# A recurrent attention step: heads 16 to 31 taken ahead of the queries of heads 0 to 15, and a filler unit dealt to four places

## The chip, the cores and the metric

The kernel runs on one core of a Trainium2 chip. The metric is the device time of one execution in microseconds; the median of three runs of the kernel before is 2796.26 us.

## The reference, cut to what matters

Four layers follow each other, A, B, A, B, each added to a residual stream of 2048 tokens by 640. The change is in layer B:

```python
for s in range(n_seg):                       # 64 segments of 32 tokens
    h = jnp.concatenate([mem, xs], axis=1)   # 8 memory tokens, 32 of the segment
    q, k, v = (jnp.einsum('btd,dhe->bhte', h, W) for W in (Wq, Wk, Wv))   # 32 heads of 128
    scores = jnp.einsum('bhqe,bhke->bhqk', q, k) * scale
    scores = jnp.where(mask[None, None], scores, -1000000000.0)
    p = _softmax(scores, axis=-1)
    o = jnp.einsum('bhqk,bhke->bhqe', p, v)
    o = jnp.einsum('bhte,hed->btd', o, Wo)
    mem = o[:, :M, :].copy()                 # the next segment's memory
```

The segments depend on each other through `mem`, so the 64 steps of a layer run one after the other.

## The kernel before

**What a step projects.** Step s of layer B works with 32 columns: the 8 memory tokens of segment s and the first 24 tokens of segment s+1. `thin_mm` multiplies them with half of a weight matrix (16 heads, 2048 columns): 5 chunks of the model dimension times 4 column tiles of the array, 20 matmuls with 32 stationary columns and 512 moving ones. A step has six such groups: Ka and Qa (keys and queries of heads 0 to 15), Kb and Qb (heads 16 to 31), Va and Vb. The last 8 tokens of each segment, its tail, are projected ahead for eight segments at a time: `tail_unit` multiplies 8 heads' weights (128 stationary columns, whole array) with 64 tail tokens, 5 matmuls a head and 40 a unit, and one unit is done in each step for a later group of segments. `tail_evac` (ScalarE) scales and writes it out to a table in HBM, `b_QKd`, from which `tails_load` takes a segment's tails back a step ahead; GpSimd (`tails_copy`) puts them into `QZ` and `KT`. `vtail_unit` and `vtail_evac` do the same for values in 20 thin matmuls, through `b_VTd`.

**From projections to scores.** `kq` evacuates a projection from PSUM to SBUF (ScalarE for Ka, Kb and Qb, VectorE for Qa), `transp4` turns it by four full-array matmuls against the identity (tiles b_TPak, b_TPaq, b_TPbk, b_TPbq), and two copies spread it: `scatter` on VectorE takes the 8 memory columns into `KT[s]` or `QT[s]`, `x_scatter` on ScalarE the 24 others into those of step s+1. `mask_mm` starts a score tile with the additive mask (one full-array matmul). There are two tiles: SPa (b_SP0) with 8 groups of 40 keys, 0 to 3 for the tail queries of all 32 heads, 4 to 7 for heads 0 to 15, and SPb (b_SP1) with groups 8 to 11 for heads 16 to 31. `scores` adds 16 matmuls for heads 0 to 15, 32 small ones for the tail queries, 16 for heads 16 to 31.

**Softmax and after.** Maxima, subtraction, sums, reciprocal and the products `Px` run on VectorE, the exponentials on ScalarE, `Pm` on GpSimd. TensorE meanwhile does Va, Vb, sometimes the LayerNorm transposes of a later block (`ln_spread`, b_lntps), and 30 matmuls of the tail unit. Then `p_transp` turns the probabilities (b_PTP), 10 more tail matmuls follow, `pv` multiplies with the values (b_OTP), `o_mm` with the output weights (b_OPS, and b_OPSd for rows put off from earlier segments, in two parts before and behind b_OPS). The new memory goes through `b_msb` (ScalarE) and b_MT (TensorE) into the 8 memory columns of `b_HX` of the next step (VectorE), with vtail matmuls between.

**Order and buffers.** The order of instructions on TensorE, ScalarE, VectorE and GpSimd is that of the program text: `_OrdNC` ties each instruction to the one before on its engine. SyncE, which starts the transfers, is not tied. PSUM has eight banks: pool `pp` has five buffers in rotation for all tiles made by `ps_tile`, pool `po` one each for the tags tail, ops and opsd. b_TPbq uses the tail buffer of `po`, as does the tail unit later in the step. Line 101 is the wrapper in `_OrdNC` through which every instruction of layer B goes, so the profile's rows are told apart by tiles.

Of the kernel before, what the change touches and what calls it, by code (L numbers as in the profile page):

```python
# [18 lines left out]
F32 = mybir.dt.float32  # L19
BF16 = mybir.dt.bfloat16  # L20
ACT = mybir.ActivationFunctionType
ALU = mybir.AluOpType
AX = mybir.AxisListType
# [6 lines left out]
NCH = 5  # L30
# [568 lines left out]
def layer_B(nc, tc, C, W, x_src, xb_src, x_dst, mem0, B_Wv, B_Wo, nsteps=64, out_bf16=False, tag=""):  # L599
    SCB = 1.0 / math.sqrt(128.0)  # L600
    nc_raw = nc
    nc = _OrdNC(tc, nc_raw, engines=ORDER_ENGINES)
    NG = nsteps // 4
    NT = nsteps // 8
    QKd = tc.dram_tile([nsteps, 128, 512], BF16, name=f"b_QKd{tag}")
    VTd = tc.dram_tile([nsteps, 8, 4096], BF16, name=f"b_VTd{tag}")
    with ExitStack() as ctx:
# [19 lines left out]
        po = psum("b_po", 1)  # L627

        def ps_tile(shape, dtype, name):
            return pp.tile(shape, dtype, name=name, tag="ps")  # L630
# [80 lines left out]
                return HXz[:, :, 0, :]  # L711
            return HX[u // 4][:, :, u % 4, :]

        def thin_mm(cols_ap, Wt, b, name):
            ps = ps_tile([128, 512], F32, name)
            for c in range(NCH):
                for j in range(4):
                    n = 4 * b + j
                    nc.tensor.matmul(ps[32 * j:32 * j + 32, :], lhsT=cols_ap[:, c, :], rhs=Wt[:, c, 512 * n:512 * n + 512],
                                     start=(c == 0), stop=(c == NCH - 1), tile_position=(0, 32 * j), skip_group_check=True)  # L720
            return ps

        def transp4(sb, name, tp=None):
            if tp is None:
                tp = ps_tile([128, 4, 128], BF16, name)
            for i in range(4):
                nc.tensor.transpose(tp[:, i, :], sb[:, 128 * i:128 * i + 128], C.identb[:])
            return tp

        def scatter(eng, tp, b, dst_t, t0, t1, c0):  # L730
            src = tp[:].rearrange("p i (j t) -> p i j t", j=4)[:, :, :, t0:t1]
            dst = dst_t[:, 16 * b:16 * b + 16, c0:c0 + (t1 - t0)].rearrange("p (j i) c -> p i j c", j=4)
            evac(eng, dst, src)
# [20 lines left out]

        tail_ps = {}

        def tail_unit(T, k, i0, i1, shared=False):
            proj, hg = divmod(k, 4)
            Wt = W.wk if proj else W.wq
            if i0 == 0:  # L760
                if shared:
                    tail_ps[0] = ps_tile([128, 8, 64], F32, "b_tail")
                else:
                    tail_ps[0] = po.tile([128, 8, 64], F32, name="b_tail", tag="tail")
            ps = tail_ps[0]
            for i in range(i0, i1):
                h = 8 * hg + i
                for c in range(NCH):
                    nc.tensor.matmul(ps[:, i, :], lhsT=Wt[:, c, 128 * h:128 * h + 128], rhs=TX[T][:, c, :, :].rearrange("p s t -> p (s t)"),
                                     start=(c == 0), stop=(c == NCH - 1))  # L770

        def tail_evac(T, k, eng, home=None):
            proj, hg = divmod(k, 4)
# [52 lines left out]
            for c in range(NCH):  # L826
                nc.sync.dma_start(HX[0][:, c, 1, 0:8], mem0[:, 128 * c:128 * c + 128].rearrange("t p -> p t"))
        for k in range(8):
            tail_unit(0, k, 0, 8, shared=True)
            tail_evac(0, k, "act" if k % 2 == 0 else "dve", (kqp, "kq"))  # L830
            if k % 4 == 1 and 2 + k // 4 < n0:
                ln_norm(2 + k // 4)
            if k % 4 == 3 and 2 + k // 4 < n0:
                ln_spread(ln_ready.pop(0))
# [21 lines left out]
            evac("act" if b == 0 else "dve", Vth[:, b, :], ps[:])  # L856
        vtails_in(0)
        if NT > 1:
            tail_unit(1, 0, 0, 8, shared=True)
            tail_evac(1, 0, "act")  # L860
            vtail_evac(1, 0, vtail_unit(1, 0), "dve")

# [51 lines left out]
        for s in range(nsteps):  # L914
# [13 lines left out]
            def x_scatter(tp, b, D_):  # L928
                if not last:
                    scatter("act", tp, b, D_[s + 1], 8, 32, 8 if D_ is KT else 0)  # L930

            def kq(ps, eng, scale=None):
                sb = kqp.tile([128, 512], BF16, name="b_kq", tag="kq")
                evac(eng, sb[:], ps[:], scale)
                return sb
# [3 lines left out]
            def mask_mm(a):  # L939
                g0, g1 = GR[a]  # L940
                SP = ps_tile([128, g1 - g0, 40], F32, f"b_SP{a}")
                nc.tensor.matmul(SP[:].rearrange("p g k -> p (g k)"), lhsT=C.identb[:], rhs=mask12[:, g0:g1, :].rearrange("p g k -> p (g k)"),
                                 start=True, stop=False, skip_group_check=True)
                return SP

            def scores(SPs):
                for b in range(2):
                    for j in range(4):
                        for i in range(4):
                            h = 16 * b + 4 * j + i  # L950
                            nc.tensor.matmul(SPs[b][32 * i:32 * i + 32, j + 4 * (1 - b), :], lhsT=QT[s][:, h, :], rhs=KT[s][:, h, :],
                                             start=False, stop=True, tile_position=(0, 32 * i), skip_group_check=True)
                    if b == 0:
                        qz = QZ[s % 2][:].rearrange("p x c -> p (x c)")
                        for j in range(4):
                            for e in range(2):
                                for t4 in range(4):
                                    pr = 8 * (t4 // 2) + 2 * j + t4 % 2
                                    nc.tensor.matmul(SPs[0][32 * t4:32 * t4 + 16, j, :], lhsT=qz[:, 24 * pr + 8 * e:24 * pr + 8 * e + 16],
                                                     rhs=KT[s][:, 2 * pr + e, :],  # L960
                                                     start=False, stop=True, tile_position=(0, 32 * t4), skip_group_check=True)

            negmax = sm.tile([128, 12], F32, name="b_negmax", tag="negmax")
            ssum = sm.tile([128, 12], F32, name="b_ssum", tag="ssum")
            rs = sm.tile([128, 12], F32, name="b_rs", tag="rs")
            E_ = wk.tile([128, 12, 40], BF16, name="b_E", tag="E0")

            def soft_max(a, SP):
                nc.vector.tensor_reduce(out=negmax[:, slice(*GR[a])], in_=SP[:], axis=AX.X, op=ALU.max, negate=True)

            def soft_sub(a, SP):
                n_ = GR[a][1] - GR[a][0]
                nc.vector.tensor_tensor(out=SP[:], in0=SP[:], in1=negmax[:, slice(*GR[a])].unsqueeze(2).to_broadcast([128, n_, 40]), op=ALU.add)

            def soft_exp(a, SP):
                nc.scalar.activation(out=E_[:, slice(*GR[a]), :], in_=SP[:], func=ACT.Exp)

            def soft_sum(a):
                nc.vector.tensor_reduce(out=ssum[:, slice(*GR[a])], in_=E_[:, slice(*GR[a]), :], axis=AX.X, op=ALU.add)

            def soft_p(eng, P_, k0, k1, g0, g1):
                eng.tensor_tensor(out=P_[:, g0:g1, 0:k1 - k0], in0=E_[:, g0:g1, k0:k1],
# [19 lines left out]
                                             tile_position=(32 * j, 0), skip_group_check=True)  # L1002


            Ka = thin_mm(cols, W.wk, 0, "b_Ka")
            ka = kq(Ka, "act")
            Qa = thin_mm(cols, W.wq, 0, "b_Qa")
            qa = kq(Qa, "dve", SCB)
            Kb = thin_mm(cols, W.wk, 1, "b_Kb")
            kb = kq(Kb, "act")  # L1010
            Qb = thin_mm(cols, W.wq, 1, "b_Qb")
            qb = kq(Qb, "act", SCB)

            TPak = transp4(ka, "b_TPak")
            scatter("dve", TPak, 0, KT[s], 0, 8, 32)
            x_scatter(TPak, 0, KT)
            TPaq = transp4(qa, "b_TPaq")
            scatter("dve", TPaq, 0, QT[s], 0, 8, 24)
            x_scatter(TPaq, 0, QT)
            TPbk = transp4(kb, "b_TPbk")  # L1020
            scatter("dve", TPbk, 1, KT[s], 0, 8, 32)
            x_scatter(TPbk, 1, KT)
            SPa = mask_mm(0)
            TPbq = transp4(qb, "b_TPbq", po.tile([128, 4, 128], BF16, name="b_TPbq", tag="tail"))
            scatter("dve", TPbq, 1, QT[s], 0, 8, 24)
            x_scatter(TPbq, 1, QT)
            SPb = mask_mm(1)
            scores((SPa, SPb))
            soft_max(0, SPa)
            soft_max(1, SPb)  # L1030
            soft_sub(0, SPa)
            soft_exp(0, SPa)
            soft_sub(1, SPb)
            soft_exp(1, SPb)
            soft_sum(0)
            soft_sum(1)
            nc.vector.reciprocal(out=rs[:], in_=ssum[:])
            soft_p(nc.vector, Px, 0, 32, 0, 8)
            soft_p(nc.gpsimd, Pm, 32, 40, 0, 12)
# [9 lines left out]
            if ln_ready:  # L1049
                ln_spread(ln_ready.pop(0))  # L1050
            if work:
                tail_unit(work[0], work[1], 0, 6)
            ptpa = p_transp(0)
            PTa = wk.tile([128, 2, 4, 40], BF16, name="b_PTa", tag="PTa")
            ptpb = p_transp(1)
# [2 lines left out]
                for pt, ptp, eng in ((PTa, ptpa, "act"), (PTb, ptpb, "dve")):  # L1058
                    evac(eng, pt[:, :, 2 * hf:2 * hf + 2, :], ptp[:, :, 2 * hf:2 * hf + 2, :])
            if work:  # L1060
                tail_unit(work[0], work[1], 6, 8)
            if unit:
                tail_evac(unit[0], unit[1], "act")
            otf = [ps_tile([128, 2, 4, 40] if j else [128, 4, 40], F32, "b_OTP") for j in range(4)]
            ots = {j: (otf[j][:, 0, :, :], otf[j][:, 1, :, :]) for j in (1, 2, 3)}
# [25 lines left out]
            def vtail_some(n_):  # L1091
                nonlocal vps, vc
                if work and vc < NCH:
                    vps = vtail_unit(work[0], work[1], vc, min(NCH, vc + n_), vps)
                    vc = min(NCH, vc + n_)

            vtail_some(2)
            if not last:
# [5 lines left out]
                for pi, (ca, cb) in enumerate(parts):  # L1104
# [6 lines left out]
                    nc.vector.tensor_copy(dst[:, ca:cb, 0:8], mt[:])  # L1111
                    vtail_some((1, 1, NCH)[pi])
            vtail_some(NCH)
            if unit:
                vtail_evac(unit[0], unit[1], vps, "act")
            if od and od["n"] == 4:
# [111 lines left out]
```

## Time and profile before

| | |
|---|---|
| runs of the kernel | 2792.15, 2796.26, 2801.13 us; median 2796.26 |
| profiled execution | 2787.25 us, span 2785.5 us, granted clock 0.981 |
| first B loop, 432 to 1365 us of the span | PE busy 918.57 of 933 us, DVE 504.28, ACT 477.55, POOL 115.66 |
| second B loop, 1803 to 2763 us | PE busy 942.08 of 960 us, DVE 515.09, ACT 486.70, POOL 121.20 |
| instructions on PE | 65414 matmuls, 65480 weight loads |
| DMA | 156.36 MB, mean 56 GB/s |

Read it so: the two B loops, 64 steps each, make up two thirds of the span. PE is TensorE; a matmul's row begins when it is issued and its end is modelled, so rows overlap, and the distance from the start of one group to the start of the next says more than the busy time. PEld are the weight loads. In the timeline each row is a group of like instructions: start, length from first start to last end, engine, line, operation, output and inputs, shapes, count, and in brackets the idle time before it with what ended it.

### The profile page before, as it was taken

The page shows a single profiled execution, that of the slowest core. Times are in us where ns is not written, and L with a number is a line of the kernel's source. Part 1 is how long each engine was busy: PE and PEld are TensorE (multiplying, and loading weights), DVE is VectorE, ACT ScalarE, POOL GpSimd, SP SyncE. Part 2 cuts the span into 40 slices and gives each one's busy share as a digit, 9 for nine tenths or more (in the row PEclk, how much of TensorE's full clock was granted, in tenths as well). Part 3 has the DMA queues.
Part 4 walks back from the last instruction along what each step waited for, and adds up shares of the span by engine and source line. Part 5 has one row for each costly group of instructions (what it writes and reads, how often), then busy time and mean ns, then how long its engine had stood idle before and what let it go on. Part 6 is the DMA issues. An engine that isn't in the chain of part 4 may idle for free. (4 is left out here: it accounts for less than half of the span.)

```text
span 2785.5 us, 146956 instructions
## 1 busy us (share of the span) xinstructions
PE 2574.7 (92%) x65414; PEld 1700.1 (61%) x65480; DVE 1686.6 (61%) x4553; ACT 1584.9 (57%) x3708; POOL 715.2 (26%) x1645
## 2 busy tenths in 40 slices
PE   5888879999999999999978888799999999999998
PEld 3555556666666666666645555556666666666665
DVE  6888854555555555555578888445555555555554
ACT  4888854555555555544458888445555455555443
POOL 4666541111111111111146665411111111111110
PEclk9999979999999999999989999899999999999999
DMA  6111162221212212111120111721211121211110
GB/s 239 41 44 40 30 195 69 45 46 41 45 43 45 43 43 45 43 39 30 41 99 28 51 49 37 231 47 39 42 42 40 40 44 40 43 41 38 39 26 20
DMA packets 322300, 156.36 MB, mean 56 GB/s; under 512 B 245760, under 2 KB 310400, under 8 KB 318592
## 3 DMA queue, kind: packets, MB, share of 16 engines
q1 hardware_dynamic: 320224, 136.47, 19.2%
q8 instruction: 512, 8.39, 1.3%
q10 hardware_dynamic: 1440, 10.49, 1.0%
q14 instruction: 124, 1.02, 0.1%
HBM read 95.15 MB, written 51.71 MB: 53 GB/s over the span
## 5 line engine op out<-in xcount | busy, mean ns | idle before, releaser
L101 PEld LDWEIGHTS <-b_HX 128*32 128x32 bf16 x15360 | 430.2, 97 | 341.0 <-issue 14.1
L101 POOL TENSOR_TENSOR b_Pm<-b_E,b_rs 128x96 bf16<-128x96 bf16 x128 | 63.3, 495 | 1443.2 <-ACT b_Vth L101 1094.2
L400 DVE TENSOR_REDUCE a_nm<-a_S 128x2 f32<-128x1024 f32 (+3 forms) x512 | 396.5, 815 | 51.4 <-PE a_T L101 26.6
L442 ACT ACTIVATE a_PT<-a_T 128x1024 bf16<-128x1024 f32 (+1 forms) x384 | 325.4, 889 | 84.9 <-PE a_T L101 50.6
L101 PE MATMUL b_OPS<-b_wo,b_OTsb 128*32 128x320 bf16 x8192 | 308.0, 301 | 10.3 <-issue 8.5
L101 PEld LDWEIGHTS <-b_OTsb 128*32 128x32 bf16 x8192 | 200.5, 97 | 97.0 <-DVE b_OTsb L101 24.1
L101 DVE CAST b_HX<-b_MT 128x8 bf16<-128x8 f32 x372 | 63.7, 172 | 277.5 <-PE b_MT L101 272.2
L444 POOL TENSOR_SCALAR_AFFINE_SELECT a_PT<-a_PT 128x256 bf16<-128x256 bf16 (+1 forms) x384 | 193.5, 520 | 143.2 <-ACT a_PT L442 141.0
L101 ACT CAST b_msb<-b_OPS 128x64 bf16<-128x64 f32 x378 | 69.3, 256 | 237.7 <-PE b_OPS L101 237.7
L101 ACT CAST b_kq<-b_Kb 128x512 bf16<-128x512 f32 x128 | 74.9, 585 | 201.6 <-PE b_Kb L101 201.6
L101 DVE COPY b_KT<-b_TPak 128x128 bf16<-128x128 bf16 x128 | 28.8, 225 | 227.0 <-PE b_TPak L101 227.0
L101 PE MATMUL b_Va<-b_wv,b_HX 128*32 128x512 bf16 x2520 | 160.8, 380 | 0.0
L101 PE MATMUL b_Vb<-b_wv,b_HX 128*32 128x512 bf16 x2520 | 160.1, 379 | 0.0
L101 PEld LDWEIGHTS <-b_kq 128*128 128x128 bf16 x2080 | 116.8, 98 | 68.8 <-ACT b_kq L101 55.6
L101 PE MATMUL b_Ka<-b_wk,b_HX 128*32 128x512 bf16 x2520 | 158.8, 379 | 0.0
L101 DVE TENSOR_SCALAR b_kq<-b_Qa 128x512 bf16<-128x512 f32 x128 | 88.5, 691 | 115.9 <-PE b_Qa L101 112.9
L101 PE MATMUL b_Kb<-b_wk,b_HX 128*32 128x512 bf16 x2520 | 158.6, 379 | 0.0
L101 PE MATMUL b_Qb<-b_wq,b_HX 128*32 128x512 bf16 x2520 | 158.6, 379 | 0.0
L101 PE MATMUL b_Qa<-b_wq,b_HX 128*32 128x512 bf16 x2520 | 158.6, 379 | 0.0
L101 DVE CAST b_OTsb<-b_OTP 128x160 bf16<-128x160 f32 (+1 forms) x384 | 122.3, 374 | 39.6 <-PE b_OTP L101 39.6
L101 PE MATMUL b_vtail<-b_wv,b_TX 128*32 128x256 bf16 x2880 | 137.7, 271 | 6.6 <-issue 3.5
L101 ACT ACTIVATE b_E<-b_SP 128x320 bf16<-128x320 f32 (+1 forms) x256 | 81.1, 368 | 109.0 <-PE b_Va L101 95.3
(195 smaller groups left out, 5764.8 us busy)
## 6 DMA issues: line engine op xcount, KB each, us to landing
b_QKd<-b_tu SPq DMA_DIRECT2D x128, 128.0 KB
b_tl<-b_QKd SPq DMA_DIRECT2D x128, 128.0 KB
b_wv<-in_B_Wv_dram SPq DMA_DIRECT2D x10, 1024.0 KB
b_wo<-in_B_Wo_dram SPq DMA_DIRECT2D x16, 640.0 KB
b_VTd<-b_vt SPq DMA_DIRECT2D x256, 32.0 KB
b_Vth<-b_VTd SPq DMA_DIRECT2D x512, 16.0 KB
b_XO<-xres SPq DMA_DIRECT2D x256, 30.0 KB
b_wk<-in_B_Wk_dram ACTq DMA_DIRECT2D x5, 1024.0 KB
```

The lines of the kernel that those rows point to most:

```text
L101: r = f(*a, **k)
L400: nc.vector.tensor_reduce(out=nm[:, qc, 2 * pr:2 * pr + 2], in_=X[:, :, o:o + w_], axis=AX.X, op=ALU.max, negate=True)
L442: nc.scalar.activation(out=PT[:, :, b:b + width], in_=Y[:, :, 0:width], func=ACT.Exp, scale=SC)
L444: nc.gpsimd.affine_select(out=dv, in_=dv, pattern=[[0, 2], [0, diag], [1, 128]], compare_op=ALU.is_ge, fill=0.0, base=0, channel_multiplie ...
```

## The change

The order of a step's front is rewritten:

- Qb, Kb and Ka are projected first (Qb evacuated by VectorE, Kb and Ka by ScalarE). b_TPbq and b_TPbk are turned and spread, SPb is begun with its mask. Qa is projected in two parts, chunks 0 and 1 before the scores of heads 16 to 31 and chunks 2 to 4 behind them (`thin_mm` takes a range of chunks and a PSUM tile). Maximum and subtraction of SPb follow at once, its exponential on ScalarE behind the evacuation of Qa, which moves to ScalarE.
- Then come b_TPak, the mask of SPa, the first 5 tail matmuls, b_TPaq, the tail scores and the scores of heads 0 to 15.
- The softmax of SPa is taken in two halves (groups 0 to 3 and 4 to 7): two maxima, subtractions, exponentials and sums where there was one of each.
- `tail_unit` counts matmuls instead of heads. With TCUT = (5, 20, 32) the 40 matmuls lie in four places: 5 before b_TPaq, 15 before `p_transp`, 12 before `pv`, 8 at the step's end behind vtail. `tail_evac` moves from before `pv` to that place, ahead of `vtail_evac`.
- b_TPbq lies in the rotation of five buffers instead of the tail buffer.

```diff
+    TCUT = (5, 20, 32)
...
-        def tail_unit(T, k, i0, i1, shared=False):
+        def tail_unit(T, k, n0, n1, shared=False):
...
-            for i in range(i0, i1):
+            for n_ in range(n0, n1):
+                i, c = divmod(n_, NCH)
                 h = 8 * hg + i
-                for c in range(NCH):
-                    nc.tensor.matmul(ps[:, i, :], lhsT=Wt[:, c, 128 * h:128 * h + 128], ...
+                nc.tensor.matmul(ps[:, i, :], lhsT=Wt[:, c, 128 * h:128 * h + 128], ...
...
-            Ka = thin_mm(cols, W.wk, 0, "b_Ka")
-            ka = kq(Ka, "act")
-            Qa = thin_mm(cols, W.wq, 0, "b_Qa")
-            qa = kq(Qa, "dve", SCB)
-            Kb = thin_mm(cols, W.wk, 1, "b_Kb")
-            kb = kq(Kb, "act")
-            Qb = thin_mm(cols, W.wq, 1, "b_Qb")
-            qb = kq(Qb, "act", SCB)
-
+            Qb = thin_mm(cols, W.wq, 1, "b_Qb")
+            qb = kq(Qb, "dve", SCB)
+            Kb = thin_mm(cols, W.wk, 1, "b_Kb")
+            kb = kq(Kb, "act")
+            Ka = thin_mm(cols, W.wk, 0, "b_Ka")
+            ka = kq(Ka, "act")
+            TPbq = transp4(qb, "b_TPbq")
+            scatter("dve", TPbq, 1, QT[s], 0, 8, 24)
+            x_scatter(TPbq, 1, QT)
+            TPbk = transp4(kb, "b_TPbk")
+            scatter("dve", TPbk, 1, KT[s], 0, 8, 32)
+            x_scatter(TPbk, 1, KT)
+            SPb = mask_mm(1)
+            Qa = thin_mm(cols, W.wq, 0, "b_Qa", 0, 2)
+            scores(1, SPb)
+            soft_max(8, 12, SPb[:])
+            soft_sub(8, 12, SPb[:])
+            thin_mm(cols, W.wq, 0, "b_Qa", 2, NCH, Qa)
+            qa = kq(Qa, "act", SCB)
             TPak = transp4(ka, "b_TPak")
             scatter("dve", TPak, 0, KT[s], 0, 8, 32)
+            SPa = mask_mm(0)
+            if work:
+                tail_unit(work[0], work[1], 0, TCUT[0])
+            soft_exp(8, 12, SPb[:])
             x_scatter(TPak, 0, KT)
             TPaq = transp4(qa, "b_TPaq")
             scatter("dve", TPaq, 0, QT[s], 0, 8, 24)
             x_scatter(TPaq, 0, QT)
-            TPbk = transp4(kb, "b_TPbk")
...
-            SPa = mask_mm(0)
-            TPbq = transp4(qb, "b_TPbq", po.tile([128, 4, 128], BF16, name="b_TPbq", tag="tail"))
...
-            SPb = mask_mm(1)
-            scores((SPa, SPb))
-            soft_max(0, SPa)
-            soft_max(1, SPb)
-            soft_sub(0, SPa)
-            soft_exp(0, SPa)
-            soft_sub(1, SPb)
-            soft_exp(1, SPb)
-            soft_sum(0)
-            soft_sum(1)
+            tail_scores(SPa)
+            scores(0, SPa)
+            soft_max(0, 4, SPa[:, 0:4, :])
+            soft_max(4, 8, SPa[:, 4:8, :])
+            soft_sub(0, 4, SPa[:, 0:4, :])
+            soft_exp(0, 4, SPa[:, 0:4, :])
+            soft_sub(4, 8, SPa[:, 4:8, :])
+            soft_exp(4, 8, SPa[:, 4:8, :])
+            soft_sum(8, 12)
+            soft_sum(0, 4)
+            soft_sum(4, 8)
...
-                tail_unit(work[0], work[1], 0, 6)
+                tail_unit(work[0], work[1], TCUT[0], TCUT[1])
...
-                tail_unit(work[0], work[1], 6, 8)
-            if unit:
+                tail_unit(work[0], work[1], TCUT[1], TCUT[2])
+            if unit and TCUT[2] == 40:
                 tail_evac(unit[0], unit[1], "act")
...
             vtail_some(NCH)
+            if work and TCUT[2] < 40:
+                tail_unit(work[0], work[1], TCUT[2], 40)
+            if unit and TCUT[2] < 40:
+                tail_evac(unit[0], unit[1], "act")
             if unit:
                 vtail_evac(unit[0], unit[1], vps, "act")
```

More of the change, by code (lines that the diff above doesn't have):

```diff
@@ L712, in cols_of, with thin_mm @@
             return HX[u // 4][:, :, u % 4, :]
-        def thin_mm(cols_ap, Wt, b, name):
-            ps = ps_tile([128, 512], F32, name)
-            for c in range(NCH):
+        def thin_mm(cols_ap, Wt, b, name, c0=0, c1=NCH, ps=None):
+            if ps is None:
+                ps = ps_tile([128, 512], F32, name)
+            for c in range(c0, c1):
                 for j in range(4):
@@ L755, in layer_B @@
         tail_ps = {}
-        def tail_unit(T, k, i0, i1, shared=False):
+        def tail_unit(T, k, n0, n1, shared=False):
             proj, hg = divmod(k, 4)
             Wt = W.wk if proj else W.wq
-            if i0 == 0:
+            if n0 == 0:
                 if shared:
@@ L765, in tail_unit @@
             ps = tail_ps[0]
-            for i in range(i0, i1):
+            for n_ in range(n0, n1):
+                i, c = divmod(n_, NCH)
                 h = 8 * hg + i
-                for c in range(NCH):
-                    nc.tensor.matmul(ps[:, i, :], lhsT=Wt[:, c, 128 * h:128 * h + 128], rhs=TX[T][:, c, :, :].rearrange("p s t -> p (s t)"),
-                                     start=(c == 0), stop=(c == NCH - 1))
+                nc.tensor.matmul(ps[:, i, :], lhsT=Wt[:, c, 128 * h:128 * h + 128], rhs=TX[T][:, c, :, :].rearrange("p s t -> p (s t)"),
+                                 start=(c == 0), stop=(c == NCH - 1), skip_group_check=True)
         def tail_evac(T, k, eng, home=None):
@@ L828, in layer_B @@
         for k in range(8):
-            tail_unit(0, k, 0, 8, shared=True)
+            tail_unit(0, k, 0, 40, shared=True)
             tail_evac(0, k, "act" if k % 2 == 0 else "dve", (kqp, "kq"))
@@ L858, in layer_B @@
         if NT > 1:
-            tail_unit(1, 0, 0, 8, shared=True)
+            tail_unit(1, 0, 0, 40, shared=True)
             tail_evac(1, 0, "act")
@@ L944, in mask_mm, with scores, tail_scores @@
                 return SP
[L946 to L961, printed above, removed]
+            def scores(b, SP):
+                for j in range(4):
+                    for i in range(4):
+                        h = 16 * b + 4 * j + i
+                        nc.tensor.matmul(SP[32 * i:32 * i + 32, j + 4 * (1 - b), :], lhsT=QT[s][:, h, :], rhs=KT[s][:, h, :],
+                                         start=False, stop=True, tile_position=(0, 32 * i), skip_group_check=True)
+            def tail_scores(SP):
+                qz = QZ[s % 2][:].rearrange("p x c -> p (x c)")
+                for j in range(4):
+                    for e in range(2):
+                        for t4 in range(4):
+                            pr = 8 * (t4 // 2) + 2 * j + t4 % 2
+                            nc.tensor.matmul(SP[32 * t4:32 * t4 + 16, j, :], lhsT=qz[:, 24 * pr + 8 * e:24 * pr + 8 * e + 16],
+                                             rhs=KT[s][:, 2 * pr + e, :],
+                                             start=False, stop=True, tile_position=(0, 32 * t4), skip_group_check=True)
             negmax = sm.tile([128, 12], F32, name="b_negmax", tag="negmax")
@@ L966, in layer_B, with soft_max, soft_sub, soft_exp @@
             E_ = wk.tile([128, 12, 40], BF16, name="b_E", tag="E0")
[L968 to L979, printed above, removed]
+            def soft_max(g0, g1, SP):
+                nc.vector.tensor_reduce(out=negmax[:, g0:g1], in_=SP, axis=AX.X, op=ALU.max, negate=True)
+            def soft_sub(g0, g1, SP):
+                nc.vector.tensor_tensor(out=SP, in0=SP, in1=negmax[:, g0:g1].unsqueeze(2).to_broadcast([128, g1 - g0, 40]), op=ALU.add)
+            def soft_exp(g0, g1, SP):
+                nc.scalar.activation(out=E_[:, g0:g1, :], in_=SP, func=ACT.Exp)
+            def soft_sum(g0, g1):
+                nc.vector.tensor_reduce(out=ssum[:, g0:g1], in_=E_[:, g0:g1, :], axis=AX.X, op=ALU.add)
             def soft_p(eng, P_, k0, k1, g0, g1):
@@ L1019, in layer_B @@
             x_scatter(TPaq, 0, QT)
-            TPbk = transp4(kb, "b_TPbk")
-            scatter("dve", TPbk, 1, KT[s], 0, 8, 32)
-            x_scatter(TPbk, 1, KT)
-            SPa = mask_mm(0)
-            TPbq = transp4(qb, "b_TPbq", po.tile([128, 4, 128], BF16, name="b_TPbq", tag="tail"))
-            scatter("dve", TPbq, 1, QT[s], 0, 8, 24)
-            x_scatter(TPbq, 1, QT)
-            SPb = mask_mm(1)
-            scores((SPa, SPb))
-            soft_max(0, SPa)
-            soft_max(1, SPb)
-            soft_sub(0, SPa)
-            soft_exp(0, SPa)
-            soft_sub(1, SPb)
-            soft_exp(1, SPb)
-            soft_sum(0)
-            soft_sum(1)
+            tail_scores(SPa)
[9 more added lines that the diff above has]
+            soft_sum(4, 8)
             nc.vector.reciprocal(out=rs[:], in_=ssum[:])
```

## The prediction

> **What bounds the kernel now.** I read the page's engine totals first, then the windows over the two B layers, then the timeline of one B step, TensorE alone and then the engines that feed it.
>
> ```profile
> PE 2574.7 (92%) x65414; PEld 1700.1 (61%) x65480; DVE 1686.6 (61%) x4553; ACT 1584.9 (57%) x3708; POOL 715.2 (26%) x1645
> ```
> ```profile
> 432.00:1365.00 933.00, 918.57 (x26937) 607.31 (x26937) 504.28 (x1576) 477.55 (x1252) 115.66 (x322) 1.00 0.20 42
> ```
>
> In the loop of the first B layer PE is busy for 918.57 of 933 us at clock 1.00, the vector and scalar engines for about half. So a step is the length of PE's sequence: what PE issues, plus where it waits. Matmul records overlap, so the waits are read from starts. From one b_Ka group to the next, 126 step lengths have a mean of 15.00 us; undisturbed ones are 14.67 to 14.71. The step at 943.57 is one of these:
>
> ```profile
> 946.80 1.25 PE L101 MATMUL b_Qb<-b_wq,b_HX 128*32 128x512 bf16 x20
> 947.99 0.40 PE L101 MATMUL b_TPak<-c_identb,b_kq 128*128 128x128 bf16 x4
> ...
> 948.82 0.40 PE L101 MATMUL b_TPbq<-c_identb,b_kq 128*128 128x128 bf16 x4
> 949.05 0.23 PE L101 MATMUL b_SP<-b_mask,c_identb 128*128 128x160 bf16 x1
> 949.21 0.28 PE L101 MATMUL b_SP<-b_KT,b_QT 128*32 128x40 bf16 x16
> ...
> 949.70 1.27 PE L101 MATMUL b_Va<-b_wv,b_HX 128*32 128x512 bf16 x20
> 950.79 1.27 PE L101 MATMUL b_Vb<-b_wv,b_HX 128*32 128x512 bf16 x20
> 951.99 1.05 PE L101 MATMUL b_tail<-b_TX,b_wq 128*128 128x64 bf16 x30
> 953.04 0.25 PE L101 MATMUL b_PTP<-c_identb,b_Px 128*128 128x128 bf16 x2
> ...
> 953.57 0.45 PE L101 MATMUL b_tail<-b_TX,b_wq 128*128 128x64 bf16 x10
> 953.96 0.52 PE L101 MATMUL b_OTP<-b_PTa,b_Vth 32*128 32x40 bf16 x32
> 954.37 0.41 PE L101 MATMUL b_OTP<-b_PTb,b_Vth 32*128 32x40 bf16 x32
> 954.71 0.46 PE L101 MATMUL b_OPSd<-b_wo,b_OTdef 128*32 128x320 bf16 x8
> ```
>
> Three things are to be seen. A 20-matmul projection takes 1.08 us start to start (54 ns each); before a full-array group it is 1.19 (Qb to TPak) and 1.20 (Vb to tail). So **a switch** from 32-column tiles to the full array costs 0.11. The way back costs 0.09: the 160-wide mask takes 0.16 to the scores, and by the 320-wide one (0.15 to its next) it should take 0.07. Second, single tail matmuls start 29 ns apart, so 30 are done 0.87 after 951.99 and PTP waits 0.18 for the softmax; the four PTP pairs take 0.53, with waits for Pm and the second Px. Third, the front, Ka to Va, has no wait: 6.13 us of issue. Each transposed group (0.23) covers the evacuation that the next needs.
>
> The weight loads show the switch too:
>
> ```profile
> 943.52 4.04 PEld L101 LDWEIGHTS <-b_HX 128*32 128x32 bf16 x80
> 947.98 0.67 PEld L101 LDWEIGHTS <-b_kq 128*128 128x128 bf16 x12 [0.42 <-ACT b_kq L101]
> ```
>
> The load before TPak idles 0.42, though its first data (ka, evacuated from 944.92 in 0.58) lay ready 2.5 us; in the step at 1003.43, where ka, qa and kb were all ready by 1007.53, the load at 1007.86 idles the same 0.42.
>
> **The change, in PE's order.** t=0 is the first matmul of the step, now Qb. PE's work is the same (40 tail matmuls, 120 thin ones, the same transposes and scores); what changes is where it waits or switches.
>
> *Front.* Qb, Kb, Ka: 3.24. Switch 0.11, TPbq at 3.35 (qb evacuated by DVE by about 2.0; every fourth step two deferred-output additions precede it there, about 2.9, still in time), TPbk 3.57, mask b 3.80. Way back to thin tiles 0.09: first 8 Qa matmuls at 3.96 (0.43). Scores b at 4.39: DVE copies TPbq 0.43 after its start (as 948.42 after 947.99) for 0.23, TPbk after it, by 4.25: in time. Then 12 Qa matmuls, 4.53 to 5.18. Switch, TPak 5.29, mask a 5.51, 5 tail matmuls, 5.66 to 5.81. TPaq needs qa: ACT starts 1.37 after the start of a 20-matmul projection (948.17 after 946.80), 0.29 after the last issue, so at 5.47; it takes 0.60, and PE sees it 0.05 later (948.77 to 948.82): 6.12. **PE waits 0.31.** Before, the same latency (0.94) lay under TPak, TPaq, TPbk and the mask; now under 0.63. ACT is free then: its last TPbk copy ends at about 4.9.
>
> TPaq ends at 6.34, way back 0.09, tail scores 6.43 to 6.67. Scores a need DVE's copy of TPaq: 6.12+0.43+0.23+0.05 = 6.83, **another wait of 0.16**; Va at 6.96. The front grows by 0.83: 0.15 tail work, 0.20 for one extra pair of switches, 0.47 waits.
>
> *Middle.* What is gained is here. Max, sub and exp of heads 16 to 31 are done in the front. From scores a (ending 6.83+0.32): max 7.24 (0.09 later, as now), sub of the first half 7.47 (160-wide rows follow each other by 0.23), exp 7.90, second exp 8.13 to 8.43, last sum 8.47, reciprocal 0.34 later as now, first Px 0.26 on, ready 9.50, seen 9.56. PE gets there at 6.96+2.29 (Va, Vb, switch)+15x0.029 = 9.69: no wait. The added exp and sums (three groups for two, 0.3 us each) are off PE's path. Pm on POOL ends at 9.70, second Px at 9.85, so the four pairs take 0.40, to 10.09; 12 tails to 10.44. PV's fourth matmul needs a PSUM buffer that PTa's second copy frees at 10.66 (now it starts about 0.17 after the first three); PTb ends at 10.83, second PV group 10.88, OPSd 11.22. From Va that is 4.26 instead of 5.01: 0.38 is moved tail work, **0.37 are waits removed.**
>
> *End.* From OPSd to the next step 3.53 us, dense now (the last vtail group is followed by Ka in 0.11), hence 14.75. The 8 tails between vtail and the next Qb cost 0.23 of moved work and two more switches, 0.20: next step at **15.18 against 14.67.** No wait is there to be filled: the next projection's first weights are loaded before the last vtail group ends.
>
> *Other queues.* The tail evacuation on ACT moves ahead of vtail's, and its store into b_QKd on SP goes from mid-step to 0.8 into the next, ahead of the b_VTd and x stores: 0.38 of SP issue, with b_XO loads then due 10 us later. Taken at nothing. If the b_tl load that reads b_QKd were late by its whole transfer, POOL's copies at about 9.6 would still precede their reader, the next step's tail scores.
>
> *The sum.* 0.20 + 0.47 - 0.37 + 0.20, with rounding 0.51 a step, x126 = 64 us. The profiled execution took 2787.25 (span 2785.5), the median of the runs is 9.0 more: 2851 for the former, **2860** for the latter.
>
> *Bounds.* A new switch: 0 to 0.12 each (in no row is a 64-wide full matmul followed by thin ones undisturbed; nearest the mask row, 0.09, which I take). TPaq wait 0.2 to 0.4, by how ACT's queue stands. Removed waits 0.25 to 0.45.
>
> On switches the Trainium skill speaks on both sides. "TensorEngine Tiling (Array Packing)", Key Properties, says that changing the tiling mode drains TensorE: by that rule, which speaks against this change, the four are paid, as in the sum, and the rows at 947.99 and 951.99 agree. "TensorE: Matmul & The Clock Gate", in its part on packing small matmuls, says that weight loads are pulled ahead of running matmuls into background weights; by that rule the new switches could be free, the second rival below. The 0.42 row speaks against it.
>
> **Rivals.**
> *Late vtail buffer (slower still).* PSUM's pool has 5 buffers, so Kb reuses the one of b_vtail. Its evacuation now queues on ACT behind b_tu: b_tu starts 0.16 into the step, vtail's copy 0.50 later, done 1.03, seen 1.08, when Kb starts. Every 0.1 late costs 13 us; with 0.1 to 0.2: 2873 to 2886. For it: no margin; against: ACT has nothing else there.
> *Free switches.* Without the four, 0.11 a step: 2810. For it: within one tile form weights do run ahead; against: the rows above.
> *Fetch stalls absorbed (faster).* The waits list puts PE's waits in OPS, OPSd, vtail and MT to "issue" (8.5, 5.8, 3.5, 3.7 us). The mean step is 0.33 over the undisturbed one, 41 us in all; 7 belong to 24 steps with LayerNorm transposes (0.29 each), 34 to such stalls. If PE's new pauses let instructions run ahead, up to 34 us return. This decides once the undisturbed step grows by less than 0.27; with free switches (0.11) it gives 2776. Against: the stretch with the stalls lies behind the new pauses and stays as dense, and so far undisturbed steps grow twice that.
> *Not doing what it says.* If exp of b ran only behind other ACT work, nothing changes: in ACT's order it stands behind qa at 5.97, still 2 us ahead of the next exp; so no chance of its own.
>
> **How the numbers follow.** Sum as worked out 0.66, late buffer 0.12, free switches 0.12, stalls absorbed 0.10. About 0.3% (8 us) is what a measurement of this kernel tells from no change; the free-switch case with some gain reaches into that, so same is 0.05, faster 0.10, slower 0.85. The range goes from 2795 (free switches, half the stalls absorbed) to 2890 (all bounds high: 0.51+0.08+0.10+0.05 = 0.74 a step). The sum's own range is 2835 to 2885.
>
> **What would show it.** Undisturbed steps from Qb to Qb of 15.1 to 15.3; TPaq 0.6 after mask a, half of it a wait; b_PTP without its 0.18 wait; Va to OPSd about 4.3; b_tail x8 followed by Qb 0.3 later. It is wrong if TPaq follows its tails at once, if thin and full groups alternate without a gap, or if the step stays under 14.9.

## The result, and the profile after

The changed kernel takes 2956.27 us (median; 2954.88 to 2957.56), the kernel before beside it 2795.41. The ratio is 1.0573 with a 95% interval of 1.0554 to 1.0592. The direction was forecast; the size was not: 161 us more where 64 were expected, outside the range that ended at 2890.

First the engine totals of the page after, then the window over the first B loop (wall time, PE, PEld, DVE, ACT, POOL busy, clock, DMA).

```profile
PE 2662.2 (90%) x65480; PEld 1659.0 (56%) x65480; DVE 1751.0 (59%) x4937; ACT 1607.3 (54%) x3836; POOL 717.7 (24%) x1645
```
```profile
436.00:1448.00 1012.00, 956.12 (x26952) 586.61 (x26955) 536.81 (x1766) 489.00 (x1315) 116.16 (x322) 1.00 0.18 39
```

PE's clock is unchanged (1.00), its busy time in the loop grew by 38 us and the loop's wall time by 79. From Qb to Qb the 126 step lengths have a mean of 16.29 us (15.00 before), the undisturbed ones 16.04 (14.67). The timeline of TensorE in the undisturbed step at 1071.19:

```profile
1073.36 1.25 PE L101 MATMUL b_Ka<-b_wk,b_HX 128*32 128x512 bf16 x20
1074.55 0.40 PE L101 MATMUL b_TPbq<-c_identb,b_kq 128*128 128x128 bf16 x4
...
1076.83 0.31 PE L101 MATMUL b_tail<-b_TX,b_wq 128*128 128x64 bf16 x5
1077.30 0.40 PE L101 MATMUL b_TPaq<-c_identb,b_kq 128*128 128x128 bf16 x4 [0.15 <-ACT b_kq L101]
1077.62 0.37 PE L101 MATMUL b_SP<-b_KT,b_QZ 128*16 128x40 bf16 x32
1078.01 0.28 PE L101 MATMUL b_SP<-b_KT,b_QT 128*32 128x40 bf16 x16
1078.13 1.25 PE L101 MATMUL b_Va<-b_wv,b_HX 128*32 128x512 bf16 x20
...
1080.39 0.61 PE L101 MATMUL b_tail<-b_TX,b_wq 128*128 128x64 bf16 x15
1081.60 0.24 PE L101 MATMUL b_PTP<-c_identb,b_Px 128*128 128x128 bf16 x2 [0.60 <-DVE b_Px L101]
...
1083.27 0.46 PE L101 MATMUL b_OPSd<-b_wo,b_OTdef 128*32 128x320 bf16 x8
...
1086.69 0.28 PE L101 MATMUL b_vtail<-b_wv,b_TX 128*32 128x256 bf16 x4
1086.91 0.41 PE L101 MATMUL b_tail<-b_TX,b_wq 128*128 128x64 bf16 x8
1087.24 1.26 PE L101 MATMUL b_Qb<-b_wq,b_HX 128*32 128x512 bf16 x20
```

Two things are to be seen. The front and the end are as forecast: TPaq waits for qa, a tail group at the end has 0.1 on either side. But the 15 tail matmuls before PTP end 0.44 after 1080.39, and PTP starts 1.21 after it. The 0.18 that PE waited there before were to vanish; they became 0.77. The waits list of TensorE over the first loop (us in total, times, longest) puts it first:

```profile
PE b_PTP L101 <- DVE b_Px L101: 34.9, 62, 1.0
PE b_TPaq L101 <- ACT b_kq L101: 9.6, 61, 0.4
```

In the same list of the kernel before, its row is:

```profile
PE b_PTP L101 <- DVE b_Px L101: 1.0, 4, 0.3
```

Why Px is late stands in the same step's timeline of VectorE:

```profile
1078.37 0.56 DVE L101 TENSOR_REDUCE b_negmax<-b_SP 128x4 f32<-128x160 f32 x2 [0.41 <-PE b_SP L101]
1079.03 0.33 DVE L101 TENSOR_TENSOR b_SP<-b_SP,b_negmax 128x160 f32<-128x160 f32 x1
1079.79 0.33 DVE L101 TENSOR_TENSOR b_SP<-b_SP,b_negmax 128x160 f32<-128x160 f32 x1 [0.43 <-ACT b_E L101]
```

and of ScalarE:

```profile
1079.46 0.30 ACT L101 ACTIVATE b_E<-b_SP 128x160 bf16<-128x160 f32 x1 [0.98 <-PE b_Va L101]
1080.16 0.30 ACT L101 ACTIVATE b_E<-b_SP 128x160 bf16<-128x160 f32 x1 [0.40 <-DVE b_SP L101]
```

The halves take turns: subtraction, exponential, subtraction, exponential. The second subtraction touches groups 4 to 7 alone and the first exponential reads groups 0 to 3, yet the one starts 0.03 after the other's end (1079.76). Both halves lie in SPa, one PSUM tile. The packed trace shows what holds it: the second subtraction waits for semaphore 110, which the first exponential raises at 1079.77. So the wait stands in the program as it was built, though the kernel's text asks for none. The first subtraction is held too: it starts 0.10 after the second maximum's end (1078.93), on its own engine, though that maximum reads the other half.

The kernel before has SPa and SPb in two tiles, and there the same work overlaps:

```profile
950.47 0.72 DVE L101 TENSOR_TENSOR b_SP<-b_SP,b_negmax 128x320 f32<-128x320 f32 x2
951.08 0.63 ACT L101 ACTIVATE b_E<-b_SP 128x320 bf16<-128x320 f32 x2 [0.77 <-PE b_Va L101]
951.55 0.71 DVE L101 TENSOR_REDUCE b_ssum<-b_E 128x8 f32<-128x320 bf16 x2 [0.35 <-ACT b_E L101]
```

The exponential of SPa starts at 951.08, before the second subtraction, that of SPb, ends at 951.19.

### The profile page after: what moved, and what is told of

Same layout as the page of the kernel before. It is cut to its first block, busy times and chain, and to the rows that moved or that the text cites. A ratio compares the mean times of both kernels' runs of the same rounds, so it can differ in the third digit from the quotient of the medians.

```text
span 2955.8 us, 147477 instructions
## 1 busy us (share of the span) xinstructions
PE 2662.2 (90%) x65480; PEld 1659.0 (56%) x65480; DVE 1751.0 (59%) x4937; ACT 1607.3 (54%) x3836; POOL 717.7 (24%) x1645
## 4 chain that ended last, share of the span: by engine, by line
PE 40%; DVE 10%; ACT 7%; issue 3%; DMA 1%; POOL 1%; SPq 0%; ACTq 0%; DVEq 0%; POOLq 0%
PE b_OPS L101 7%; PE b_Qa L101 4%; PE b_Qb L101 3%; PE b_Kb L101 3%; PE b_Ka L101 3%; ACT a_PT L442 3%; PE b_SP L101 2%; DVE b_ssum L101 2%; PE b_OTP L101 2%; PE b_tail L101 2%; DVE b_SP L101 2%; PE b_PTP L101 2%; PE b_OPSd L101 2%; ACT b_kq L101 2%; PE b_vtail L101 2%
## 5 line engine op out<-in xcount | busy, mean ns | idle before, releaser
L101 PEld LDWEIGHTS <-b_HX 128*32 128x32 bf16 x15360 | 365.5, 96 | 338.0 <-issue 9.8
L101 ACT ACTIVATE b_E<-b_SP 128x160 bf16<-128x160 f32 x384 | 115.8, 302 | 181.1 <-PE b_Va L101 112.4
L101 DVE TENSOR_REDUCE b_negmax<-b_SP 128x4 f32<-128x160 f32 x384 | 112.8, 322 | 122.5 <-PE b_SP L101 122.5
L101 PE MATMUL b_Qa<-b_wq,b_HX 128*32 128x512 bf16 x2520 | 171.7, 380 | 0.0
L101 DVE TENSOR_TENSOR b_SP<-b_SP,b_negmax 128x160 f32<-128x160 f32 x384 | 127.8, 333 | 73.5 <-ACT b_E L101 55.4
L101 ACT CAST b_OTsb<-b_OTP 128x320 bf16<-128x320 f32 x256 | 96.5, 429 | 110.6 <-PE b_OTP L101 110.6
L101 DVE COPY b_QT<-b_TPbq 128x128 bf16<-128x128 bf16 x128 | 28.8, 225 | 210.0 <-PE b_TPbq L101 210.0
```

Of the source, the lines that this page charges most:

```text
L101: r = f(*a, **k)
```

## The experiments

**My theory** after the result: instructions on the two halves of one PSUM tile wait for each other, and that is the whole of the error; the rest of the sum (switches, waits in the front) stands. **Rivals:** three short groups with changes of engine are dear in themselves; the loss lies in the front; switches cost nothing. The kernel before was run again beside each batch: 2784.16 us beside the first four experiments, 2791.56 beside the next four, 2790.12 beside the last. The ratios go by these.

**Two tiles.** SPa is parted into two tiles in different banks; the heads' half lies in the bank that b_OPS uses later in the step.

```diff
-            GR = ((0, 8), (8, 12))
+            GR = ((0, 4), (8, 12), (4, 8))
...
+                if a == 2:
+                    SP = po.tile([128, g1 - g0, 40], F32, name="b_SPh", tag="ops")
...
             SPa = mask_mm(0)
+            SPh = mask_mm(2)
...
-            scores(0, SPa)
+            scores(0, SPh)
...
-            soft_sub(4, 8, SPa[:, 4:8, :])
-            soft_exp(4, 8, SPa[:, 4:8, :])
...
+            soft_sub(4, 8, SPh[:])
+            soft_exp(4, 8, SPh[:])
```

> The changed kernel with SPa in two PSUM tiles (tail groups in one, heads 0 to 15 in one of another bank) and two masks. Undisturbed steps of the changed kernel are 16.04 us, PTP starts 10.40 into them. Theory: instructions on the two halves of one PSUM tile wait for each other; apart, the second subtraction starts without waiting for the first exponential, PTP is at 9.6 to 9.7, steps are 15.15 to 15.3 and the time near 2850. Rival: three short groups with a change of engine in each cost this much anyway; then PTP stays at 10.3 to 10.4, steps at 16.0, time at 2950.

Measured: 2840.74 us, ratio to the kernel before 1.021 (1.0154 to 1.0266); undisturbed steps 15.14, PTP at 9.64. VectorE in the step at 1066.33 of this kernel:

```profile
1073.24 0.33 DVE L101 TENSOR_REDUCE b_negmax<-b_SP 128x4 f32<-128x160 f32 x1
1073.50 0.32 DVE L101 TENSOR_REDUCE b_negmax<-b_SPh 128x4 f32<-128x160 f32 x1
1073.75 0.32 DVE L101 TENSOR_TENSOR b_SP<-b_SP,b_negmax 128x160 f32<-128x160 f32 x1
1073.98 0.32 DVE L101 TENSOR_TENSOR b_SPh<-b_SPh,b_negmax 128x160 f32<-128x160 f32 x1
```

and ScalarE:

```profile
1074.16 0.30 ACT L101 ACTIVATE b_E<-b_SP 128x160 bf16<-128x160 f32 x1 [0.56 <-DVE b_SP L101]
1074.39 0.30 ACT L101 ACTIVATE b_E<-b_SPh 128x160 bf16<-128x160 f32 x1
```

and TensorE:

```profile
1075.52 0.61 PE L101 MATMUL b_tail<-b_TX,b_wq 128*128 128x64 bf16 x15
1075.97 0.24 PE L101 MATMUL b_PTP<-c_identb,b_Px 128*128 128x128 bf16 x2
```

The same instructions now follow each other every 0.23 to 0.26 us on both engines. The first maximum no longer waits for the scores of the other half either, the first subtraction starts (1073.75) before the second maximum has ended (1073.82), and PTP follows the 15 tail matmuls after 0.45, without a wait. That is 0.90 us a step, two thirds of the growth of 1.37. The edit parts the tile and the bank at once, so it doesn't tell which of the two the wait goes by.

**One piece.** In the changed kernel, the softmax of SPa is put back into one piece of 8 groups.

```diff
-            soft_max(0, 4, SPa[:, 0:4, :])
-            soft_max(4, 8, SPa[:, 4:8, :])
+            soft_max(0, 8, SPa[:])
...
-            soft_sum(0, 4)
-            soft_sum(4, 8)
+            soft_sum(0, 8)
```

> The changed kernel with the softmax of SPa in one piece of 8 groups, as before the change. Theory of the halves that wait for each other: PTP at 10.0 instead of 10.40, steps 15.65 to 15.7, time near 2910. Rival: splitting in halves helps and the loss lies elsewhere; then PTP comes later than 10.40 and the time is 2956 or more.

Measured: 2902.09, ratio 1.0431 (1.0399 to 1.0462), PTP at 10.09, steps 15.73. PTP and steps are a little above what was expected. Splitting inside one tile is worse than not splitting, by 0.31 a step.

**No tail work at the end.**

```diff
-    TCUT = (5, 20, 32)
+    TCUT = (5, 28, 40)
```

> The changed kernel with TCUT = (5, 28, 40): the 8 tail matmuls of the step's end go in front of PTP, where PE waits 0.74 for the softmax; tail_evac goes back before pv. Theory: a pair of switches between 32-column tiles and the full array costs 0.2, so steps fall by 0.43 (0.23 work into a wait, 0.20 switches) to 15.6, time near 2902. Rival: a switch costs nothing; steps fall by 0.23 to 15.8, time near 2927.

Measured: 2903.48, ratio 1.0436 (1.0399 to 1.0473); PTP stays at 10.38, steps 15.58, 0.46 less. The eight tails are 0.23 of it (8 at 29 ns), so the two switches are 0.23.

**The end alone, in the kernel before.**

```diff
-                tail_unit(work[0], work[1], 0, 6)
+                tail_unit(work[0], work[1], 0, 22)
...
+            if work:
+                tail_unit(work[0], work[1], 32, 40)
             if unit:
+                tail_evac(unit[0], unit[1], "act")
                 vtail_evac(unit[0], unit[1], vps, "act")
```

(The 10 matmuls ahead of `pv` are 22 to 31; `tail_evac` there is taken out.)

> The kernel before with the tail unit dealt 22 before PTP, 10 before pv, 8 at the step's end behind vtail, and tail_evac there; nothing else changed. PTP is held by the softmax at 9.48 and should stay. Theory of dear switches: steps 14.68 + 0.23 + 0.20 = 15.1, time near 2850. Rival of free switches: 14.9, time near 2825.

Measured: 2829.53, ratio 1.017 (1.0123 to 1.0217); PTP at 9.49, steps 15.12. TensorE at the end of a step:

```profile
1072.57 0.28 PE L101 MATMUL b_vtail<-b_wv,b_TX 128*32 128x256 bf16 x4
1072.78 0.41 PE L101 MATMUL b_tail<-b_TX,b_wq 128*128 128x64 bf16 x8
1073.12 0.83 PE L101 MATMUL b_Ka<-b_wk,b_HX 128*32 128x512 bf16 x12
```

In the kernel before, Ka follows that vtail group after 0.11; here the tails follow after 0.21, and Ka starts 0.34 after them for 0.23 of work. So each way costs 0.10 to 0.11, also from the 64-wide full matmuls, which no undisturbed row of before had shown. The steps fit the theory, but the time lies nearer the rival's 2825 than the theory's 2850: the mean step of this run is 15.31, only 0.31 above that of the kernel before, where the undisturbed one grew by 0.45.

**The split alone, in the kernel before.** SPa in halves, in its one tile; order of heads as before.

```diff
-            soft_sub(0, SPa)
-            soft_exp(0, SPa)
+            soft_sub(2, SPa[:, 0:4, :])
+            soft_exp(2, SPa[:, 0:4, :])
+            soft_sub(3, SPa[:, 4:8, :])
+            soft_exp(3, SPa[:, 4:8, :])
```

(Maxima and sums likewise.)

> The kernel before with one part of the change alone: the softmax of SPa (8 groups, one PSUM tile) in two halves, two maxima, subtractions, exponentials and sums. Theory of halves that wait for each other in one tile: the second subtraction waits for the first exponential, PTP moves from 9.48 to 9.85 to 9.9 of the step, steps from 14.68 to 15.05 to 15.1, time about 50 us up. Rival (the wait needs the changed order of the queues): PTP and steps within 0.1 of the kernel before.

Measured: 2856.49, ratio 1.0228 (1.0198 to 1.0259); PTP at 9.84, steps 15.04, the time 65 us above the kernel before beside it, where about 50 were expected. VectorE's timeline has the same mark:

```profile
1017.18 0.32 DVE L101 TENSOR_TENSOR b_SP<-b_SP,b_negmax 128x160 f32<-128x160 f32 x1
1017.95 0.56 DVE L101 TENSOR_TENSOR b_SP<-b_SP,b_negmax 128x160 f32<-128x160 f32 x2 [0.45 <-ACT b_E L101]
```

So the wait needs nothing of the new order; the split in one tile brings it into the old order too.

**Two tiles, and tail work in the front's wait.** The kernel of the first experiment with other cuts.

```diff
-    TCUT = (5, 20, 32)
+    TCUT = (15, 28, 40)
```

> The kernel with SPa in two tiles, TCUT = (15, 28, 40): no tail matmuls at the end, 10 more ahead of TPaq. Theory: the ten lie in the 0.3 that PE waits there for the evacuation of Qa, so TPaq stays at 6.10; the end loses 0.43; PTP stays at 9.6; steps 14.7, as the kernel before, time within 10 us of it. Rival: TPaq is not waiting for Qa but for the transposes' own path; then it moves by 0.29 to 6.4 and steps are 15.0.

Measured: 2796.3, ratio 1.0014 (0.9998 to 1.003); TPaq stays at 6.09 with ten more matmuls ahead of it, steps 14.68. With the halves apart, the end free and the wait filled, the new order comes out level with the old one.

**A dense front, heads 16 to 31 first.** From the two-tile kernel: Qa in one piece, all projections, then all transposes, three masks, three score groups.

```diff
+            Qa = thin_mm(cols, W.wq, 0, "b_Qa")
+            qa = kq(Qa, "act", SCB)
             TPbq = transp4(qb, "b_TPbq", po.tile([128, 4, 128], BF16, name="b_TPbq", tag="tail"))
...
             TPak = transp4(ka, "b_TPak")
...
+            SPb = mask_mm(1)
             TPaq = transp4(qa, "b_TPaq")
...
+            SPh = mask_mm(2)
+            scores(1, SPb)
             tail_scores(SPa)
             scores(0, SPh)
```

(Maximum, subtraction and exponential of SPb move behind the scores, ahead of the others. Tail unit 22 before PTP, 18 before `pv`; no tail work in the front or at the end.)

> All four projections and four transposes in one go (Qb, Kb, Ka, Qa; TPbq, TPbk, TPak, two masks, TPaq, third mask), then scores of heads 16 to 31, tail, heads 0 to 15; each of the three in a PSUM tile of its own, softmax in three groups of four; tail unit 22 ahead of PTP, 18 ahead of pv. Theory: the front is as dense as before the change (Va at 6.13), nothing waits across tiles, PTP comes at 9.05 to 9.15, steps 14.2 to 14.3, time 2 to 3% below the kernel before. Rival (three short groups cost more than they bring): PTP at 9.4 or later, no gain.

Measured: 2763.69, ratio 0.9893 (0.9873 to 0.9913). Va at 6.16, PTP at 9.10, as said; steps 14.39, more than said, since the 18 tail matmuls and the switch to `pv` take 0.62 after PTP, of which I had left the switch out. The time is 1.1% below the kernel before, not 2 to 3.

**The same with SPa in one tile and one piece**, tail unit 30 and 10.

```diff
-            scores(0, SPh)
+            scores(0, SPa)
...
-            soft_max(0, 4, SPa[:])
-            soft_max(4, 8, SPh[:])
+            soft_max(0, 8, SPa[:])
```

(The other softmax operations likewise.)

> The same dense front with SPa in one tile and its softmax in one piece, tail unit 30 and 10. Theory: Va at 6.13, PTP at 9.35 to 9.4, steps 14.55 to 14.6, time 0.5 to 1% below the kernel before. Rival: order of heads alone brings nothing; steps 14.7.

Measured: 2784.42, ratio 0.9973 (0.9957 to 0.9988); PTP at 9.39, steps 14.59, the time 0.3% below, less than expected. This order of heads, with its changed evacuation engines, brings 0.08 a step.

**Three tiles, order of heads as before.** The kernel before with SPa in two tiles as in the first experiment, softmax in three groups, tail unit 22 and 18.

```diff
             SPa = mask_mm(0)
+            SPh = mask_mm(2)
...
+            order3 = ((2, SPh), (0, SPa), (1, SPb))
+            for a, SP in order3:
+                soft_max(a, SP)
+            for a, SP in order3:
+                soft_sub(a, SP)
+                soft_exp(a, SP)
+            for a, SP in order3:
+                soft_sum(a)
```

> The kernel before with its order of heads, projections and transposes, SPa in two PSUM tiles (three groups of four with SPb, softmax in three parts), tail unit 22 and 18. Theory: the order of heads is nearly without effect and the tiles do it: Va at 6.15, PTP at 9.1, steps 14.4, time 1% below the kernel before, as with the dense front of three tiles (0.9893). Rival: heads 16 to 31 first is what brings PTP forward; then PTP at 9.35 or later and a gain under 0.5%.

Measured: 2760.89, ratio 0.9891 (0.9876 to 0.9906); Va 6.16, PTP 9.10, steps 14.39, each the same as with heads 16 to 31 first. With the dense front of three tiles it is the fastest kernel tried here, and it changes less. The order of heads is without effect once the tiles are apart. What the new deal of the tail unit (22 and 18) brings by itself was not tried.

## Why the prediction was wrong

Medians over undisturbed steps, us from the step's start:

| point | predicted | changed kernel | the same, two tiles |
|---|---|---|---|
| TPbq | 3.35 | 3.35 | 3.35 |
| TPaq | 6.12 | 6.10 | 6.10 |
| Va | 6.96 | 6.93 | 6.93 |
| PTP | 9.69 | 10.40 | 9.64 |
| OPSd | 11.22 | 12.07 | 11.17 |
| next Qb | 15.18 | 16.04 | 15.14 |

**The step that failed** is the softmax replay in the middle: "sub of the first half 7.47 (160-wide rows follow each other by 0.23), exp 7.90, second exp 8.13 to 8.43". The kernel before has such a spacing, but from the maximum of SPb (950.24) to the subtraction of SPa (950.47), two tiles. No softmax row of before had a write to one part of a PSUM tile beside a read of another, and the price of that should have been bounded from both sides. It was taken at nothing. In the changed kernel's step the subtraction waits for both maxima (7.84), the exponentials come at 8.27 and 8.97, the second 0.84 later than written. PTP then waits, and "0.37 are waits removed" became 0.51 added: Va to OPSd takes 5.14 where 5.01 less the 0.38 of tail work moved out were due. With the tiles apart, the replay is right within 0.05 at every point of the table.

Rows of before came near the price. Parts of one SBUF tile are free: ScalarE's second exponential writes groups 8 to 11 of b_E until 951.71, and VectorE sums groups 0 to 7 of it from 951.55. Parts of one PSUM tile look otherwise: VectorE copies 8 columns of each transposed group and ScalarE the 24 others, and in none of 126 steps do the two copies of b_TPak overlap; at 948.68 ScalarE starts 0.03 after VectorE's end, and its copy waits for a semaphore (100) that VectorE's copy raises at 948.66. ScalarE was busy until about then, so no idle time showed it. The changed kernel shows it as a wait, in front of b_TPaq, between two engines that both only read:

```profile
1077.73 0.23 DVE L101 COPY b_QT<-b_TPaq 128x128 bf16<-128x128 bf16 x1 [0.61 <-PE b_TPaq L101]
1077.99 0.48 ACT L101 COPY b_QT<-b_TPaq 128x384 bf16<-128x384 bf16 x1 [0.18 <-DVE b_QT L101]
```

A rule for this can be read, too. The Trainium skill, "PSUM — Partial Sum Buffer", section "PSUM bank collisions raise a hardware error", says that the hardware doesn't arbitrate when two engines touch a PSUM bank at once, and that accesses are to be guarded by bank and quadrant (32 partitions) rather than by address. By that rule VectorE may not write one half while ScalarE reads the other, since both halves lie in all 128 partitions. The trace fits it: 0.43 of waiting with both halves in one tile, none with two. It doesn't cover the first subtraction, which waits for a maximum of its own engine. Whether the chip itself would have objected isn't shown: the program's semaphores kept the accesses apart, and no run here puts the two halves into two tiles of one bank.

**The other terms.** Front: right to 0.03, both waits (0.31 and 0.16) included; ten matmuls put into the first cost nothing. Switches: 0.20 a pair forecast, 0.23 and 0.22 measured (the third and fourth experiments: 0.46 and 0.45 less 0.23 of work). End: 3.96 forecast from OPSd, 3.97 measured. On the switches, the rule that the prediction names from the Trainium skill, "TensorEngine Tiling (Array Packing)", Key Properties, that a change of tiling mode drains TensorE, fits these prices; the pulling ahead of weight loads did not make the switches free.

**The rivals.** Late vtail buffer: Kb starts 1.09 into the step, and the first loop's waits list has 0.4 us for it in all; no loss. Free switches: refuted by the rows at the step's end (0.10 and 0.11). Fetch stalls absorbed: partly so. The mean step lies 0.25 over the undisturbed one instead of 0.33, so about 10 us came back (172 by undisturbed steps, 162 by the mean). Over the experiments this excess goes from 0.17 (one piece) to 0.45 (the split alone), so a time near a forecast says less than the undisturbed step. Why it changes wasn't tried.

The error is thus closed. It is 0.86 a step, 16.04 instead of 15.18: PTP comes 0.71 late, and from PTP to OPSd it takes 1.67 instead of 1.53, since Pm and the second Px come late as well and the four PTP pairs take 0.53 instead of 0.40. With two tiles both are gone. The growth of 1.37 over the kernel before parts another way: 0.90 for halves in one tile and 0.46 for the end, of which 0.43 was forecast. What the front pays beyond that and the waits removed about cancel: with two tiles, no tail work at the end and the front's wait filled, steps are 14.68.

## What to carry to other kernels

Before a piece is split so that two engines can overlap on it, give each part a PSUM tile in a bank of its own: in one tile the split here cost 0.31 us a step more than no split, in two it gained 0.59. In a replay of a step, bound every pair of neighbouring instructions that has no row yet, also where they only share a PSUM tile. Filler matmuls belong where TensorE waits and beside groups of their own tile form; eight of them between groups of another form, at a dense place, cost their own 0.23 and as much again.

## What the runs showed of the hardware

At a granted clock of 1.00, a change between 32-column tiles and the full array costs 0.09 to 0.11 us each way, whether the streams before it are 512, 256, 160 or 64 wide. Two 160-wide instructions of VectorE on different tiles start 0.23 to 0.26 us apart, a dependent one on the same tile 0.03 to 0.10 after the end of the first. VectorE's and ScalarE's accesses to parts of one PSUM tile, kept apart by the program's semaphores, did not overlap in the split score tile (changed kernel) nor in b_TPak and b_TPaq; their accesses to parts of one SBUF tile (b_E) did, in all 128 steps of the kernel before.
